# Attention and channel mix on one core: an order made by a small planner, q transposed two tokens at a time, kv kept in both partition halves, and two-bank PSUM tiles

## The chip, the cores and the metric

The kernel runs on one core of one Trainium2 chip. The metric is device time in microseconds (us), the median of several executions. A profiled execution gives a trace; its span (first to last instruction) is about 2 us shorter than the device time. "PE" is the matmul engine, "PEld" its weight loads, "DVE" VectorE, "ACT" ScalarE, "POOL" GpSimd, which issues the loads here. "Clock" is the TensorE clock that the throttle granted, as a share of full speed.

## The reference, cut to what matters

Batch 8, 8 heads, 576 tokens, 64 numbers a head. All of a batch's attention is linear: one 64x64 matrix `kv` a head, then `q @ kv`, normalised.

```python
kv = np.einsum('bhsd,bhse->bhde', k, v)
out = np.einsum('bhsd,bhde->bhse', q, kv)
rms = np.sqrt(np.mean(out * out, axis=-1, keepdims=True) + 1e-06)
x = (out / rms * g_norm)            # then heads side by side: [8, 576, 512]
x_prev = x shifted by one token
xk = mu_k * x + (1 - mu_k) * x_prev # xr likewise with mu_r
k = np.maximum(xk @ w_k, 0.0)       # 512 -> 1024
v = k * k @ w_v                     # 1024 -> 512
out = sigmoid(xr @ w_r) * v
```

## The kernel before

The kernel works on two kinds of things at once. *Attention* of a batch b (576 tokens) is a long chain: kv product, transposes of q, `u` (q times kv), squares, `st` (sum of squares), Ln and Exp on ScalarE, `rr` (spreads 1/rms over partitions), product with u, difference with the shifted token, blends to xk and xr. *Channel mix* of a group g (512 tokens) is 80 large matmuls: 32 for k, 16 for r (the gate), 32 for v. Group g needs x of batch g (and of those before it).

The attention matmuls use half the array's columns or rows:

```python
def transposes(hp):                  # hp: a pair of heads
    ps = psa.tile([128, S], BF16, tag="at", name="ps_qt")
    for j in range(NJ):              # NJ = 6 tokens a partition, NP = 96
        for e in range(2):
            nc.tensor.transpose(ps[64*e:64*e+64, NP*j:NP*j+NP],
                qin[:, 2*hp+e, HD*j:HD*j+HD], ident[:NP, :NP])
    nc.scalar.copy(out=st["qT"][:, hp, :], in_=ps)

def u(hp):
    for half in range(2):
        cs = slice(HS*half, HS*half+HS)          # HS = 288
        ps = psa.tile([128, HS], FP32, tag="at", name="ps_u")
        for e in range(2):
            es = slice(64*e, 64*e+64)
            nc.tensor.matmul(ps[es], st["kv"][es, hp, :], st["qT"][es, hp, cs], ...)
        nc.scalar.copy(out=st["uT"][:, hp, cs], in_=ps)
```

PSUM is two pools of four one-bank tiles, `psm` for the channel mix and `psa` for attention. The order on each engine is the order of the Python calls: every group has 20 units (r and k first, then v) and a table puts attention steps of a later batch after certain units:

```python
front(1, 0, [0, 1, 2, 3, 4])   # batch 1: kv after unit 0 of group 0, transposes after units 1 to 4
rest(1, 0, 5)
for b in range(2, B):
    front(b, b - 2, [15, 16, 17, 18, 19])
    rest(b, b - 1, 2)
```

In the trace, an instruction that has to wait holds up those behind it on its engine: in the first stretch shown below PE stands 3.3 us before one product although others could run.

## Time and profile before

| | before |
|---|---|
| time, median of its three runs by then (248.6, 252.0 and a slow one of 421.6) | 252.0 us |
| span of the profiled run, its clock | 250.2 us, 0.952 |
| first k product of group 1 | 66.7 us |
| period (one batch of attention and one group) | 24.5 us |

The head of the profile page of the kernel before: busy time of each engine, its share of the span, and its number of instructions.

```profile
span 250.2 us, 4403 instructions
## 1 busy us (share of the span) xinstructions
PE 218.7 (87%) x1746; PEld 93.2 (37%) x1746; DVE 154.6 (62%) x302; ACT 136.0 (54%) x252; POOL 23.6 (9%) x38
```

PE is the engine to look at. Two stretches of its timeline carry the argument. The columns are start in us, duration in us, engine, line, operation, what it writes and reads, shapes, number of matmuls merged, and in brackets the idle time before and what ended it. The start of the kernel before:

```profile
27.12 2.79 PE L229 MATMUL ps_r<-w_r,xr 128*128 128x512 bf16 x4 [3.49 <-DVE xr L202]
33.18 1.49 PE L141 MATMUL ps_kv<-vin,kin 96*64 96x64 bf16 x48 [3.27 <-DMA vin<-in_v_dram]
34.60 1.89 PE L229 MATMUL ps_r<-w_r,xr 128*128 128x512 bf16 x4
36.42 0.69 PE L125 MATMUL ps_qt<-ident,qin 96*64 96x96 bf16 x12
...
39.23 1.04 PE L229 MATMUL ps_r<-w_r,xr 128*128 128x512 bf16 x4
```

After four gate products PE comes to batch 1's kv product and waits 3.3 us for its data, although twelve more gate products could run.

A period in the steady state of the kernel before:

```profile
109.39 0.95 PE L141 MATMUL ps_kv<-vin,kin 96*64 96x64 bf16 x48
110.27 1.04 PE L242 MATMUL ps_v<-w_v,sqk 128*128 128x512 bf16 x4
111.24 0.45 PE L125 MATMUL ps_qt<-ident,qin 96*64 96x96 bf16 x12
111.62 1.04 PE L242 MATMUL ps_v<-w_v,sqk 128*128 128x512 bf16 x4
...
118.35 0.43 PE L159 MATMUL ps_u<-qT,kv 64*64 64x288 bf16 x4
118.71 1.04 PE L219 MATMUL ps_km<-xk,w_k 128*128 128x512 bf16 x4
```

Starts are more useful than durations, since matmuls overlap: a block of twelve transposes costs 0.38 us (111.24 to 111.62), a block of u 0.36, and the four large matmuls after either cost 0.97, where four undisturbed ones cost 0.86 (16 in 3.45 us in the last stage).

### The profile page before, as it was taken

The numbers are of one execution on the slowest core, as the hardware profiler recorded it, in microseconds if no ns is written. First come the engines' busy times: TensorE is split into PE (matmuls) and PEld (weight loads), VectorE is DVE, ScalarE is ACT, GpSimd is POOL, SyncE is SP. The second block draws the span as 40 slices with busy tenths as digits, with TensorE's granted clock in tenths as the row PEclk, the third lists the DMA queues.
The fourth block names the chain that finished last, engine by engine and source line by source line (L and its number), as shares of the span: only waits on it lengthen the run. The fifth ranks groups of instructions, "written<-read, shape, count | busy, mean of one in ns | idle before, by whom it ended". The sixth has DMA issues, their size and how long they took to land.

```text
span 250.2 us, 4403 instructions
## 1 busy us (share of the span) xinstructions
PE 218.7 (87%) x1746; PEld 93.2 (37%) x1746; DVE 154.6 (62%) x302; ACT 136.0 (54%) x252; POOL 23.6 (9%) x38
## 2 busy tenths in 40 slices
PE   0284369969998999899989998999899989999992
PEld 0251044324432543344335433543344334444440
DVE  0126920648875986597669766976796579714422
ACT  2077017850589258925891689168826880632610
POOL 8740021002100210021002100000000000000000
PEclk9997559995999999999999999999999999999999
DMA  5999999942990199019902990240023003206014
GB/s 82 182 208 207 203 203 204 203 81 54 206 182 0 42 183 226 2 45 179 230 2 55 206 197 0 56 114 0 3 83 85 4 0 85 87 9 159 1 55 113
DMA packets 26771, 26.49 MB, mean 106 GB/s; under 512 B 1656, under 2 KB 21632, under 8 KB 26752
## 3 DMA queue, kind: packets, MB, share of 16 engines
q0 software_dynamic: 20960, 16.78, 44.1%
q1 hardware_dynamic: 5792, 9.45, 13.2%
q8 instruction: 13, 0.21, 0.3%
q14 instruction: 6, 0.05, 0.1%
HBM read 33.56 MB, written 9.44 MB: 172 GB/s over the span
## 4 chain that ended last, share of the span: by engine, by line
PE 69%; ACT 15%; DMA 12%; issue 1%; DVE 1%; POOL 1%; DVEq 0%; POOLq 0%
PE ps_v L242 26%; PE ps_km L219 26%; DMA vin<-in_v_dram 9%; PE ps_r L229 5%; PE ps_qt L125 4%; PE ps_u L159 4%; ACT L176 4%; ACT L232 3%; PE ps_kv L141 3%; DMA kin<-in_k_dram 3%; ACT ln L177 3%; ACT rs L178 2%; ACT relu L222 2%; ACT sig L232 1%; DVE out_sb L247 1%
## 5 line engine op out<-in xcount | busy, mean ns | idle before, releaser
L242 PE MATMUL ps_v<-w_v,sqk 128*128 128x512 bf16 x288 | 70.0, 387 | 5.3 <-ACT sig L232 3.3
L219 PE MATMUL ps_km<-xk,w_k 128*128 128x512 bf16 x288 | 68.9, 380 | 0.0
L222 ACT ACTIVATE relu<-ps_km 128x512 bf16<-128x512 f32 x72 | 42.9, 597 | 28.9 <-PE ps_km L219 24.4
L223 DVE TENSOR_TENSOR sqk<-relu 128x512 bf16<-128x512 bf16 x72 | 30.3, 425 | 35.5 <-ACT relu L222 35.3
L130 ACT COPY qT<-ps_qt 128x576 bf16<-128x576 bf16 x32 | 20.2, 638 | 56.5 <-PE ps_qt L125 56.5
L229 PE MATMUL ps_r<-w_r,xr 128*128 128x512 bf16 x144 | 37.3, 400 | 3.9 <-DVE xr L202 3.5
L242 PEld LDWEIGHTS <-sqk 128*128 128x128 bf16 x288 | 26.2, 98 | 37.7 <-issue 7.7
L219 PEld LDWEIGHTS <-w_k 128*128 128x128 bf16 x288 | 25.2, 98 | 32.3 <-issue 6.5
L247 DVE TENSOR_TENSOR out_sb<-ps_v,sig 128x512 f32<-128x512 f32 x36 | 24.2, 686 | 16.7 <-PE ps_v L242 16.7
L232 ACT ACTIVATE sig<-ps_r 128x512 bf16<-128x512 f32 x36 | 19.6, 601 | 16.1 <-PE ps_r L229 16.0
L229 PEld LDWEIGHTS <-xr 128*128 128x128 bf16 x144 | 13.1, 100 | 24.2 <-DVE xr L202 6.0
L161 ACT CAST uT<-ps_u 128x288 bf16<-128x288 f32 x64 | 22.1, 413 | 0.0
L164 DVE TENSOR_TENSOR sq<-uT 128x576 bf16<-128x576 bf16 x32 | 14.7, 458 | 9.4 <-ACT uT L161 9.0
L190 DVE TENSOR_TENSOR xT_133<-uT,ps_rr 128x288 bf16<-128x288 bf16 x32 | 12.3, 449 | 8.9 <-PE ps_rr L187 8.8
L141 PE MATMUL ps_kv<-vin,kin 96*64 96x64 bf16 x384 | 9.4, 213 | 8.5 <-DMA vin<-in_v_dram 8.5
L190 DVE TENSOR_TENSOR xT_134<-uT,ps_rr 128x288 bf16<-128x288 bf16 x32 | 12.3, 449 | 6.7 <-PE ps_rr L187 6.7
L125 PEld LDWEIGHTS <-qin 96*64 96x64 bf16 x384 | 11.1, 119 | 14.3 <-issue 12.3
L125 PE MATMUL ps_qt<-ident,qin 96*64 96x96 bf16 x384 | 15.3, 223 | 0.9 <-DMA qin<-in_q_dram 0.8
L66 POOL DMA_DIRECT2D kin<-in_k_dram x9 | 6.9, 766 | 91.7 <-PE ps_kv L141 89.6
L159 PE MATMUL ps_u<-qT,kv 64*64 64x288 bf16 x128 | 14.6, 311 | 0.0
L141 PEld LDWEIGHTS <-kin 96*64 96x64 bf16 x384 | 8.7, 128 | 11.9 <-issue 9.5
L187 PE MATMUL ps_rr<-rs,selg 32*128 32x288 bf16 x64 | 10.8, 301 | 2.6 <-ACT rs L178 1.4
(41 smaller groups left out, 132.0 us busy)
## 6 DMA issues: line engine op xcount, KB each, us to landing
out_dram<-out_sb SPq DMA_DIRECT2D x24, 192.0 KB
kin<-in_k_dram POOLq DMA_DIRECT2D x7, 576.0 KB, 7.6
vin<-in_v_dram POOLq DMA_DIRECT2D x7, 576.0 KB, 10.6
qin<-in_q_dram POOLq DMA_DIRECT2D x7, 576.0 KB, 10.1
out_dram<-out_sb SPq DMA_DIRECT2D x24, 128.0 KB
out_dram<-out_sb SPq DMA_DIRECT2D x24, 64.0 KB
w_k<-in_moe_w_k_dram POOLq DMA_DIRECT2D x1, 1024.0 KB, 15.1
w_v<-in_moe_w_v_dram POOLq DMA_DIRECT2D x1, 1024.0 KB, 19.5
```

What stands on the lines that cost most here:

```text
L125: nc.tensor.transpose(ps[64 * e:64 * e + 64, NP * j:NP * j + NP], qin[:, 2 * hp + e, HD * j:HD * j + HD], ident[:NP, :NP],)
L141: nc.tensor.matmul(ps[64 * e:64 * e + 64, i, :], kin[:, 2 * hp + e, HD * j:HD * j + HD], vin[:, 2 * hp + e, HD * j:HD * j + HD], start=(j ...
L159: nc.tensor.matmul(ps[es], st["kv"][es, hp, :], st["qT"][es, hp, cs], start=True, stop=True)
L161: nc.scalar.copy(out=st["uT"][:, hp, cs], in_=ps)
L190: nc.vector.tensor_mul(out=xT[:, hp, NP + HS * half:NP + HS * half + HS], in0=st["uT"][:, hp, cs], in1=pss[hp])
L219: nc.tensor.matmul(ps, w_k_sb[:, cc, 128 * fc:128 * fc + 128], xk[:, cc, G * g:G * g + G], start=(cc == 0), stop=(cc == NHP - 1))
L222: nc.scalar.activation(out=rt, in_=ps, func=AF.Relu)
L223: nc.vector.tensor_mul(out=sqk[g][:, fc, :], in0=rt, in1=rt)
L229: nc.tensor.matmul(ps, xr[:, cc, n0:n0 + 128], w_r_sb[:, cc, :], start=(cc == 0), stop=(cc == NHP - 1))
L232: nc.scalar.activation(out=sig[(g, ci)], in_=ps, func=AF.Sigmoid)
L242: nc.tensor.matmul(ps, sqk[g][:, fc, 128 * ci:128 * ci + 128], w_v_sb[:, fc, :], start=(fc == 0), stop=(fc == NFC - 1))
L247: nc.vector.tensor_mul(out=ot, in0=ps, in1=sig[(g, ci)])
```

## The change

Its intent: less PE work for attention, fewer evictions, and an order that is computed, not written by hand.

- *Algebra.* q is transposed for two tokens at once (96x128, so six transposes a head pair, not twelve). The two tokens of a pair then lie in the two partition halves, so kv must stand in both halves (four small copies a batch in place of one), and u runs on four 64x64 tiles.
- *Two-bank PSUM tiles.* Two tiles for the mix and two for attention, of two banks each, so that one instruction evicts 1024 (or 576) columns.
- *Planner.* Every piece of work says which engines can do it, for how long (assumed durations), what it depends on, which buffers it needs, and a `due` number. At build the planner simulates the engines. On each it takes the piece that can start first, and among those within 0.02 us of it the one with the lowest `due`. The result is the fixed order of the instructions.
- Batch 0 is loaded and computed in three parts; xk and xr are rings of four batches.

The core of the diff, much cut:

```diff
+class Planner:
+    def run(self):
+            ...
+            for eng, c in best.items():
+                t0 = min(x[0] for x in c)
+                picks.append(min((x for x in c if x[0] <= t0 + 0.02), key=lambda x: x[1]) + (eng,))
...
+        "mm": (2, (128, 2, 512), FP32),
+        "at": (2, (128, 2, 512), FP32),
...
+        def due(x):
+            return 20 * b - 2 * x if b else -100 - x
...
+        def kv_copy(eng, e):
+            for half in range(2):
+                copy(eng, get(kv)[64 * half:64 * half + 64, hsl, e, :],
+                     pkv.t[64 * e:64 * e + 64, 0, 0:HD * n].rearrange("q (i d) -> q i d", d=HD))
...
+                for e in range(2):
+                    for i in range(NI):
+                        nc.tensor.transpose(t[:, e, NP * i:NP * i + NP],
+                                            qin.t[:, 2 * hp + e, 128 * i:128 * i + 128], ident[:NP, :NP])
...
+                for jj in range(2):
+                    js = slice(64 * jj, 64 * jj + 64)
+                    for e in range(2):
+                        nc.tensor.matmul(t[64 * e:64 * e + 64, jj, 0:NI * NP], kv.t[js, hp, e, :],
+                                         qT.t[js, 2 * hp + e, :], start=True, stop=True)
...
+        st = add({"ACT": 3.9 if b else 1.35}, st_act, deps=[m], bufs=[pst, ln, rs], due=due(17))
```

In `due(x)`, x is a number of the piece: 27 for the transposes, 26 for kv, 22 for u, 14 for rr, 10 or 6 for the blends. The mix of group g has numbers from 20g to 20g + 21.

## The prediction

> **What bounds the kernel now.** TensorE, after a slow start. On the page its busy share is 87% of the 250.2 us span; VectorE is at 62%, ScalarE at 54%. In the chain of waits PE holds 69%, ScalarE 15%, DMA 12%.
>
> Start: the chain is DMA until 33.18 us. The PE timeline shows why: gate products (L229) start at 27.1 us, but PE's next instruction is batch 1's kv product, waiting 3.3 us for its `vin`. The `ps_km` products of group 1 start only at 66.70 us.
>
> Steady state: starts of the kv product at 84.9, 109.4 and 133.9 us give a period of 24.5 us. In the last stage, without attention work, 16 large matmuls take 3.45 us (0.216 us each), so the period's 80 take 17.3 us. The rest: kv 0.88; four transposing blocks of 12 at 0.38; four u blocks at 0.36; stat 0.36; rr about 1.2; a wait for sigmoid 0.55; and after each return to 128x128 tiles a block of four costs 0.97 instead of 0.86 us, 13 times, 1.4 us. The sum is 24.6 us.
>
> **What the change does, by period.**
> - Transposes: 6 per head pair, not 12, at 96x128, so in the large matmuls' tiling mode. The Trainium skill's "TensorEngine Tiling (Array Packing)", Key Properties, says that changing mode drains TensorE; the 0.11 us above agrees. Estimate 0.28 us a block and no return cost: saves about 0.8 us.
> - u: the same four matmuls of 288 columns, but on four 64x64 tiles at once instead of two and two. Estimate 0.24 for 0.36 us: saves 0.5 us, more where two blocks are joined.
> - Fewer mode changes (about 9 returns a period, counted in the instruction order, for 13) and less stalled rr: about 1 us.
> - Added: kv is copied twice as four 64-partition pieces (1 to 2 us on ScalarE or VectorE); one group's k matmuls are split at the ring's wrap.
> - Two-bank tiles halve the number of evictions. ScalarE about 17.5, VectorE about 19 us a period (estimates from the durations of before): close, but still under PE's.
> New period: estimate 22.1 to 22.8 us.
>
> **The start.** Batch 0 is loaded and computed in three parts and batch 1's kv no longer stands before group 0's products. Loads stay bound by DMA at about 204 GB/s (batch 1 still lands at about 33 to 36 us). I expect group 0's gate products at 24 to 26 us, its k products running while batch 1 lands, and group 1's k products at about 54 us instead of 66.7. Three table loads of 1.28 us for batch 0 eat part of the gain. Before group 1 PE will still idle some 4 us, waiting for VectorE's blends.
>
> **Sum.** From 54 us: 8 groups at 17.3 plus about 5.6 attentions at 5.2 us, some 168 us, plus a tail of about 4.5 us: span about 226, time (some 2 us above the span) 227 us.
>
> Chances: faster 0.96, same 0.03, slower 0.01.
>
> **What would show it.** Transposing blocks of 6 under 0.35 us with no slow matmul after them; u blocks under 0.3 us; kv-to-kv period at 22 to 23 us; first group-1 k product between 50 and 58 us; PE busy share 88% or more.
>
> **What would make it wrong.** The order is fixed at build from assumed durations. If ScalarE or VectorE run behind them, two `mm` tiles give PE no more slack than four single ones, and PE waits for evictions; VectorE at about 85% makes this the likeliest miss (time 232 to 240). If the four u tiles do not run together, 3 to 4 us stay.

## The result

| | before | after |
|---|---|---|
| time, median of four | 251.9 us (fast runs 248.6 to 252.0, their median 251.8) | 240.5 us (239.9 to 240.6) |
| span, clock of the profiled run | 250.2 us, 0.952 | 238.5 us, 0.982 |
| first k product of group 1 | 66.7 us | 60.8 us |
| first k product of group 8, the last | 228.1 us | 214.4 us |

Ratio 0.958, 95% interval 0.950 to 0.965: faster. A ratio is the mean of one kernel's fast runs over the mean of the other's of the same rounds, so not quite the ratio of the medians. One run of before, 421.6 us, is left out of the ratio as slow. The prediction of 227 us was too low by 13.5 us.

The two mean clocks are not comparable. The trace's clock records begin at 18.3 us in the kernel before and at 31.87 us in the kernel after, and the views count time before the first record as full speed. It was not: in the kernel after the gate products run 0.43 us apart (the first two 0.73) until then and 0.216 after.

The head of the profile page of the kernel after:

```profile
span 238.5 us, 3893 instructions
## 1 busy us (share of the span) xinstructions
PE 207.4 (87%) x1586; PEld 98.0 (41%) x1586; DVE 158.7 (67%) x263; ACT 123.3 (52%) x154; POOL 25.1 (11%) x39
```

PE has 11 us less busy time, yet its share of the span is the same 87%. The PE timeline of the kernel after, in its steady state:

```profile
114.32 1.89 PE L453 MATMUL mm<-xk,w_k 128*128 128x512 bf16 x8
116.05 0.68 PE L315 MATMUL at<-ident,q 96*128 96x96 bf16 x12
117.85 0.43 PE L360 MATMUL at<-sq,sel_72 128*32 128x288 bf16 x8 [1.13 <-ACT qT L172]
...
134.53 0.32 PE L335 MATMUL at<-qT,kv 64*64 64x288 bf16 x4
134.78 1.04 PE L495 MATMUL mm<-w_v,sqk 128*128 128x512 bf16 x4
```

The new pieces cost what was predicted: u 0.25 us (134.53 to 134.78). The second fence below shows transposes of six at 0.35 us before rr, where PE changes mode (52.49 to 52.84), and four v products between transposes at 0.87 (51.62 to 52.49), so transposes in the large matmuls' shape no longer cost a change of mode. But at 117.85 PE has stood 1.13 us, until ScalarE had emptied an attention tile.

Group 0's gate products, which the prediction had at 24 to 26 us, and its first k products in the kernel after:

```profile
25.90 6.65 PE L476 MATMUL mm<-w_r,xr 128*128 128x512 bf16 x15 [1.58 <-DVE xr L413]
32.38 3.62 PE L453 MATMUL mm<-xk,w_k 128*128 128x512 bf16 x16
```

The end of the kernel's start, the PE timeline of after just before group 1's k products:

```profile
51.62 1.03 PE L495 MATMUL mm<-w_v,sqk 128*128 128x512 bf16 x4
52.49 0.42 PE L315 MATMUL at<-ident,q 96*128 96x96 bf16 x6
52.84 0.29 PE L384 MATMUL at<-rs,selg 32*128 32x288 bf16 x2
53.63 0.30 PE L384 MATMUL at<-rs,selg 32*128 32x288 bf16 x2 [0.50 <-ACT qT L172]
54.64 0.30 PE L384 MATMUL at<-rs,selg 32*128 32x288 bf16 x2 [0.71 <-DVE xT L391]
...
56.63 0.98 PE L335 MATMUL at<-qT,kv 64*64 64x288 bf16 x8 [0.21 <-DVE xT L391]
...
58.37 2.66 PE L315 MATMUL at<-ident,q 96*128 96x96 bf16 x24
60.83 1.90 PE L453 MATMUL mm<-xk,w_k 128*128 128x512 bf16 x4
```

From 52.84 to 60.83 us PE has only small pieces. It waits 2.6 us between them, and from 55.76 to 62.59 us the clock records stand at 0.50: the 24 transposes at 58.37 take 2.46 us where four blocks of six at full clock take 1.02. The window from 33 to 66 us (its columns are explained further down) has a mean clock of 0.90:

```profile
33.00:66.00 33.00, 29.56 (x348) 15.52 (x347) 22.93 (x39) 20.36 (x31) 6.92 (x9) 0.90 1.29 215
```

Batch 1's Exp was done at 48.8 us, but its rr stands in the order behind batch 2's transposes, and comes at 52.84.

*The account.* Give every block of PE from 60.83 us on its undisturbed cost: 0.2157 us a large matmul, 0.11 after a change of mode, and kv 0.88, st 0.36, transposes 0.255 a six, u 0.13 and 0.12 for every four, rr 0.11 and 0.06 for each. The sum is 164.0 us. Up to the last matmul's end it took 172.9 us. So some 9 us are lost: 7.8 us are PE's idle gaps, none above 1.13 us, and 0.9 is the slow clock in the first four k products (60.83 to 62.66). From 25.9 us on the sum is 190.0, and it took 207.9: 18 us of waits and slow clock, half of them before group 1.

VectorE in the kernel after, by windows (stretch, its length, then busy time of PE, PEld, DVE, ACT and POOL with instructions, clock, DMA share, GB/s):

```profile
66.00:99.00 33.00, 30.77 (x247) 13.40 (x245) 32.25 (x54) 22.18 (x28) 2.31 (x3) 1.00 0.75 125
```

VectorE is busy 32.25 of 33 us, 98%, though its share over the whole run is 67%. What it does there, in its timeline:

```profile
74.41 3.00 DVE L413 SCALAR_TENSOR_TENSOR xk<-d,mu_sb,xT 128x576 bf16<-128x576 bf16 x4
77.33 1.19 DVE L344 TENSOR_TENSOR sq<-uT 128x576 bf16<-128x576 bf16 x3
78.43 3.00 DVE L413 SCALAR_TENSOR_TENSOR xr<-d,mu_sb,xT 128x576 bf16<-128x576 bf16 x4
81.35 1.29 DVE L460 TENSOR_TENSOR sqk<-relu 128x1024 bf16<-128x1024 bf16 x2
82.56 1.73 DVE L174 CAST kv<-at 64x256 bf16<-64x256 f32 x4
84.45 1.42 DVE L391 TENSOR_TENSOR xT<-uT,at 128x576 bf16<-128x576 bf16 x2
```

These are blends of batch 2, squares of batch 3 and kv copies of batch 4, while group 1's v products start only at 84.56. The planner works ahead. I took from this three theories:

1. *The due numbers.* Attention's numbers make pieces of later batches go before what the current group needs.
2. *The durations* (rival). The planner assumed wrong times (for batch 0's statistics 1.35 us, measured 2.70 with the table load), so the order does not fit the chip.
3. *The evictions and the four PSUM tiles* (rival). Two two-bank tiles a kind give less slack than four single ones.

### The profile page after: what moved, and what is told of

It reads as the page before. It is cut to its first block, busy times and chain, and to the rows that moved or that the text cites. A ratio compares the mean times of both kernels' runs of the same rounds, so it can differ in the third digit from the quotient of the medians.

```text
span 238.5 us, 3893 instructions
## 1 busy us (share of the span) xinstructions
PE 207.4 (87%) x1586; PEld 98.0 (41%) x1586; DVE 158.7 (67%) x263; ACT 123.3 (52%) x154; POOL 25.1 (11%) x39
## 4 chain that ended last, share of the span: by engine, by line
PE 64%; DVE 16%; ACT 10%; DMA 5%; issue 2%; POOL 0%; SPq 0%; DVEq 0%; ACTq 0%; POOLq 0%
PE mm L495 22%; PE mm L453 22%; PE mm L476 11%; DVE out L499 4%; DMA q<-in_q_dram 3%; DVE xT L391 3%; PE at L315 2%; DMA out_dram<-out 2%; PE at L293 2%; ACT L365 2%; DVE xr L413 2%; DVE xk L413 2%; DVE sq L344 2%; ACT relu L457 2%; PE at L335 1%
## 5 line engine op out<-in xcount | busy, mean ns | idle before, releaser
L495 PE MATMUL mm<-w_v,sqk 128*128 128x512 bf16 x288 | 68.2, 380 | 1.7 <-DVE out L499 1.7
L453 PE MATMUL mm<-xk,w_k 128*128 128x512 bf16 (+1 forms) x320 | 67.6, 361 | 1.4 <-DVE out L499 1.4
L457 ACT ACTIVATE relu<-mm 128x1024 bf16<-128x1024 f32 x36 | 36.3, 1020 | 48.1 <-PE mm L453 48.1
L499 DVE TENSOR_TENSOR out<-mm,sig 128x1024 f32<-128x1024 f32 (+1 forms) x20 | 22.3, 1115 | 24.2 <-PE mm L495 17.8
L476 PE MATMUL mm<-w_r,xr 128*128 128x512 bf16 x144 | 36.5, 402 | 2.1 <-DVE xr L413 1.6
L460 DVE TENSOR_TENSOR sqk<-relu 128x1024 bf16<-128x1024 bf16 x36 | 24.6, 689 | 18.2 <-ACT relu L457 18.0
L391 DVE TENSOR_TENSOR xT<-uT,at 128x576 bf16<-128x576 bf16 (+1 forms) x31 | 21.7, 731 | 7.4 <-PE at L384 7.2
L480 ACT ACTIVATE sig<-mm 128x1024 bf16<-128x1024 f32 x18 | 18.5, 1027 | 12.0 <-PE mm L476 11.7
L413 DVE SCALAR_TENSOR_TENSOR xr<-d,mu_sb,xT 128x576 bf16<-128x576 bf16 x32 | 24.2, 813 | 0.0
L413 DVE SCALAR_TENSOR_TENSOR xk<-d,mu_sb,xT 128x576 bf16<-128x576 bf16 x32 | 24.1, 812 | 0.1
L365 ACT ACT_TABLE_LOAD x10 | 12.8, 1283 | 0.2
```

What stands on the lines that cost most here:

```text
L391: nc.vector.tensor_mul(out=xT.t[:, hs, xs], in0=get(uT)[:, hs].rearrange("q h i jj p -> q h (i jj p)")[:, :, cs], in1=ps.t[:, 0:step, 0:HS])
L413: nc.vector.scalar_tensor_tensor(out=dst[:, hp, c0:c0 + S], in0=d.t[:, hp, :], scalar=mu_sb[:, m + hp:m + hp + 1], in1=xT.t[:, hp, 0:S], o ...
L453: nc.tensor.matmul(get(ps)[:, fc % 2, a0:a1], w_k_sb[:, cc, 128 * fc:128 * fc + 128], xk[:, cc, x0:x0 + a1 - a0], start=(cc == 0), stop=(c ...
L457: nc.scalar.activation(out=get(rt), in_=ps.t, func=AF.Relu)
L460: nc.vector.tensor_mul(out=get(sqk)[:, 2 * f2:2 * f2 + 2, :], in0=rt.t, in1=rt.t)
L476: nc.tensor.matmul(get(ps)[:, ci % 2, :], xr[:, cc, n0:n0 + 128], w_r_sb[:, cc, :], start=(cc == 0), stop=(cc == NHP - 1))
```

## The experiments

All twelve were correct. K1 and K8 are the starts of the first k product of groups 1 and 8 in the profiled run. The reader may use the ratio, whose two sides come from the same chip and rounds; the kernel before ran at 250.6 to 251.9 us (medians) in the four sets of rounds, that of the result among them.

| run | time, us | ratio to before | K1 | K8 | span |
|---|---|---|---|---|---|
| before | 251.9 | 1 | 66.7 | 228.1 | 250.2 |
| after | 240.5 | 0.958 | 60.8 | 214.4 | 238.5 |
| e1_algebra_alone | 243.5 | 0.970 | 63.8 | 219.8 | 241.9 |
| e2_plan_alone | 243.3 | 0.970 | 62.0 | 217.0 | 241.1 |
| e3_later_due | 236.4 | 0.942 | 61.4 | 209.7 | 234.2 |
| e4_no_tables_b0 | 240.1 | 0.958 | 58.1 | 212.5 | 236.7 |
| e5_split_evict | 241.6 | 0.960 | 59.7 | 214.6 | 238.8 |
| e6_tail | 238.4 | 0.947 | 59.4 | 213.9 | 236.0 |
| e7_order_only | 230.5 | 0.915 | 59.3 | 205.8 | 228.0 |
| e8_all_fixes | 226.7 | 0.901 | 56.0 | 203.3 | 225.5 |
| e9_durations_alone | 239.8 | 0.956 | 57.8 | 215.4 | 239.5 |
| e10_front_alone | 236.8 | 0.943 | 61.5 | 210.4 | 234.5 |
| e11_before_start | 244.2 | 0.973 | 58.3 | 219.7 | 241.9 |
| e12_fixes_old_algebra | 230.8 | 0.919 | 56.0 | 206.6 | 228.7 |

### e1: the algebra alone

The kernel before with `transposes`, `kv` and `u` of the new kind; one-bank tiles, hand order. One kv copy goes to ScalarE, one to VectorE.

```diff
-            for j in range(NJ):
-                for e in range(2):
-                    nc.tensor.transpose(ps[64 * e:64 * e + 64, ...], qin[:, 2 * hp + e, HD * j:HD * j + HD], ...)
+            for e in range(2):
+                for i in range(NJ // 2):
+                    nc.tensor.transpose(ps[:, e, ...], qin[:, 2 * hp + e, 128 * i:128 * i + 128], ...)
```

> The kernel before, with only the new algebra: q transposed two tokens at a time, kv kept in both partition halves, u on four 64x64 tiles; old order, one-bank tiles. If the PE time that the change saves is real work off the bound engine, each of some 6.5 periods loses 4 x 0.24 us at the transposes and 4 x 0.11 us at u, about 9 us: 241 to 245 us. If the extra kv copies or waits give it back: 248 us or more.

243.5 us, as expected. Consecutive v stages start at 101.51 and 125.02 us: a period of 23.5 us against 24.5. The algebra's PE time is real, about 1 us a period.

### e2: planner and two-bank tiles alone

The kernel after with the old transposes, single kv and old u (and their durations) put back into the planner.

```diff
-                    for i in range(NI):
-                        nc.tensor.transpose(t[:, e, NP * i:NP * i + NP], qin.t[:, 2 * hp + e, 128 * i:128 * i + 128], ...)
+                for j in range(NJ): ...
+                        nc.tensor.transpose(t[64 * e:64 * e + 64, 0, NP * j:NP * j + NP],
+                                            qin.t[:, 2 * hp + e, HD * j:HD * j + HD], ...)
```

> The kernel after, with the old algebra put back into the planner (12 transposes a head pair, one kv, u two tiles at a time): planner and two-bank tiles alone. If the after kernel is bound by PE's work, the 1.4 us a period come back: 247 to 250 us. If it is bound by waits of a fixed order, the shorter attention work was partly hidden in them, and this shows only 243 to 246 us.

243.3 us: the case of waits. By medians each half of the change alone brings about 8 us, and both together 11, so they overlap by some 5. In the kernel after, the algebra is worth only 2.8 us.

### e3: later due numbers

```diff
-            return 20 * b - 2 * x if b else -100 - x
+            return 20 * b - 2 * x + 15 if b else -100 - x
```

> One constant in the after kernel: the due number of all attention pieces of batches 1 to 7 rises by 15 (three quarters of a group later). Theory: the missing time is waits that the order itself makes, because pieces of later batches go ahead of what the current group needs and VectorE saturates (98% busy from 66 to 99 us). Then 227 to 232 us, with VectorE no longer above 95% in any 33 us stretch. Rivals (durations that the planner has wrong; too few attention PSUM tiles): no change, 238 to 242 us.

236.4 us, 4 us less, but not the 9 to 13 that I expected. VectorE's window from 66 to 99 us falls to 29.57 us (90%). Starts of k products come at 84.09, 106.59, 129.08 and 151.63 us: an even period of 22.5 us. So theory 1 holds for the middle of the run, and another share of the loss lies elsewhere: K1 is at 61.4, no earlier. (VectorE's busiest 33 us are now from 55 to 88, at 31.53 us or 95.5%, just above what I expected.)

### e4: no table loads for batch 0

The table with Ln and Exp is loaded once at the very start, and batch 0 loads it three times more.

```diff
-            nc.scalar.preload_act_table_set("natural_log_exp_and_others")
+            if b:
+                nc.scalar.preload_act_table_set("natural_log_exp_and_others")
```

ScalarE's timeline in the kernel after shows what is taken away, three times in a row:

```profile
14.84 1.28 ACT L365 ACT_TABLE_LOAD   x1
16.13 0.74 ACT L366 ACTIVATE ln<-at,eps 64x576 f32<-64x576 f32 x1
16.90 0.68 ACT L368 ACTIVATE rs<-ln 64x576 bf16<-64x576 f32 x1
17.60 1.28 ACT L365 ACT_TABLE_LOAD   x1
```

> The after kernel, same order, without the three table loads (1.28 us each) in batch 0's statistics, whose table is loaded already. If the start runs through ScalarE (its chain from 14.8 to 23.1 us), group 0's gate products start about 2.5 to 3.8 us sooner than 25.9, and the end moves by 2 to 3 us: 237 to 238.5 us. If the later waits absorb it: the start moves and the end does not, 240 us.

240.1 us (238.8 to 240.7): unclear, at most a fraction of a microsecond. Gate products start only 0.6 us sooner than 25.9 (at 25.34, after one at 22.43 for 23.71), not the 2.5 to 3.8 expected. The profiled run has K1 2.7 us sooner and K8 1.9 sooner; its time was at the low end. The Trainium skill's "ScalarE: Activation LUTs", What ACT_TABLE_LOAD costs, gives about 1283 ns for the load, and the trace has exactly that mean. For a switch to another table the page adds a drain of about 1380 ns. The fence above reloads a table that is in use already, but a true switch shows no drain either: in the kernel before Exp ends at 79.37 us, the load runs from 79.40 to 80.68, and Sigmoid starts at 80.69.

### e5: the two-bank evictions undone

The same order, but relu, its square, sigmoid and output product as two one-bank instructions each.

```diff
-            nc.scalar.activation(out=get(rt), in_=ps.t, func=AF.Relu)
+            get(rt)
+            for x in range(2):
+                nc.scalar.activation(out=rt.t[:, x, :], in_=ps.t[:, x, :], func=AF.Relu)
```

> The after kernel with the same order, but every two-bank eviction of the channel mix (relu, its square, sigmoid, output product) issued as two one-bank instructions. From the mean durations (relu 2 x 597 against 1020 ns, square 2 x 425 against 689, output 2 x 686 against 1221) ScalarE gets about 9 us more work and VectorE about 8. If those engines' waits carry the time, 3 to 6 us slower than 240.5; if the joining of evictions is off the critical chain, within 1 us.

241.6 us, 1.1 more by medians and 0.2% by ratio. The joining of the channel mix's evictions is hardly on the chain. The extra busy time was also smaller than I had worked out: ScalarE 126.2 against 123.3 us, VectorE 163.1 against 158.7.

### e6: the tail

The last group evicts its output tiles in halves, but the halves share one PSUM tile. PE's timeline at the end of the kernel after:

```profile
224.72 2.75 PE L495 MATMUL mm<-w_v,sqk 128*128 128x512 bf16 x12
228.31 3.61 PE L495 MATMUL mm<-w_v,sqk 128*128 128x512 bf16 x16 [0.84 <-DVE out L499]
232.76 1.02 PE L495 MATMUL mm<-w_v,sqk 128*128 128x512 bf16 x4 [0.84 <-DVE out L499]
```

PE writes the second bank of the tile, and waits until VectorE has read the first. With a tile for each half:

```diff
-            ps, ot, u = Buf("mm"), Buf("out"), slot + 12 + 4 * c2
+            pp, ot, u = [Buf("mm")], Buf("out"), slot + 12 + 4 * c2
+            pp.append(pp[0] if g < NG - 1 else Buf("mm"))
```

> The after kernel with one PSUM tile for each 128 tokens in the last group's output product, so that PE need not wait until VectorE has read the first half of a two-bank tile (two waits of 0.84 us in the last stage, and a slice of output). Expected 1.5 to 2 us less: 238.4 to 239.

238.4 us, as expected: 2 us. In its trace the last 32 products are one block without a wait:

```profile
224.30 7.07 PE L495 MATMUL mm<-w_v,sqk 128*128 128x512 bf16 x31
```

(One record of 32 is missing from the trace.)

### e7: the order fixes together

e3, e4 and e6, and a next batch's kv and transposes less urgent than this batch's rr (the change of e10).

> Order and waits together, with the planner's assumed durations unchanged: the later due numbers (236.4 alone), no table loads in batch 0, the last group's tiles split, and a next batch's kv and transposes no longer more urgent than this batch's rr. If the missing 13 us are such waits, the gains add: group 1's k products at 57 to 58 us instead of 60.8, 230 to 232 us.

230.5 us, as expected, though K1 came later than I wrote (59.3). Waits that seemed small one by one add up to 10 us. From K1 to the last matmul's end it takes 163.7 us (59.34 to 223.03), where the kernel after takes 172.9: the 9 us lost there are gone.

### e8: the same, with durations that the trace shows

```diff
-        st = add({"ACT": 3.9 if b else 1.35}, ...
+        st = add({"ACT": 2.75 if b else 1.45}, ...
-            sigs.append((sg, add({"ACT": 1.04}, ...
+            sigs.append((sg, add({"ACT": 1.04 + 1.28 * (c2 == 0)}, ...
-            qts[hp] = add({"ACT": 0.65, "DVE": 0.75}, ...
+            qts[hp] = add({"ACT": 0.65, "DVE": 0.46}, ...
-            m = add({"PE": 0.35}, ... q_tr ...
+            m = add({"PE": 0.26}, ... q_tr ...
```

> As the run before it, and the planner is given durations that the trace shows (table load counted with sigmoid, qT copy on VectorE 0.46 us, transposes 0.26 us). Rival theory that the order is stale because its durations are wrong: 2 us or more better than the run before, group 1's k products at 54 to 56 us, 227 to 229 us. If the durations hardly matter: within 1 us of the run before.

226.7 us, ratio 0.901 (0.898 to 0.904): this version beats both kernels, and is where the prediction had put the change itself. Against e7 it gains before K1 only: from K1 to K8 it takes 147.3 us, e7 146.5. Its profiled run is the slowest of four and has 3.4 us at a clock of 0.50 (54.92 to 58.34), e7's has 6.8 (54.15 to 60.97), and the other three runs of e8 have a mean clock of 0.999 or 1.000, those of e7 0.985. So part of the 3.8 us between them is the clock; whether the better order keeps it up is not shown. Its window from 66 to 99 us, and a period of its PE timeline:

```profile
66.00:99.00 33.00, 32.52 (x258) 14.64 (x263) 29.39 (x48) 22.26 (x27) 3.08 (x4) 1.00 0.75 121
```

```profile
123.45 1.91 PE L454 MATMUL mm<-xk,w_k 128*128 128x256 bf16 x16
125.29 0.95 PE L293 MATMUL at<-v,k 96*64 96x64 bf16 x48
...
135.13 0.42 PE L315 MATMUL at<-ident,q 96*128 96x96 bf16 x6
135.39 1.03 PE L477 MATMUL mm<-w_r,xr 128*128 128x512 bf16 x4
...
145.58 0.38 PE L454 MATMUL mm<-xk,w_k 128*128 128x512 bf16 x1
```

PE is busy 32.52 of 33 us, and the period, 123.45 to 145.58, is 22.1 us. That is the predicted sum without waits.

### e9: the durations alone

The changed numbers of e8 on the kernel after (2.75 us for all statistics, since batch 0 keeps its loads), the due numbers untouched.

> The after kernel with only the planner's assumed durations corrected (table load of the statistics 2.75 us and of sigmoid 1.28 us apart, qT copy on VectorE 0.46, transposes 0.26), its due numbers as they were. If wrong durations alone made the order bad: 236 us or less. If the due numbers are the cause and right durations only help once those are right: 238 to 243 us.

239.8 us, runs from 238.7 to 241.6: no gain that the runs can tell. K1 does come 3 us sooner (57.8), but K8 is at 215.4, later than in the kernel after. (The profiled run is the slowest of the four, at a mean clock of 0.981; the two below 239 us have 0.993 and 0.999.) So theory 2 alone falls as the cause of the whole time: right durations came with 3.8 us from e7 to e8, and with nothing that can be told without the right due numbers. For the start it does not fall (see K0 below).

### e10: one priority

```diff
-        mm = add({"PE": 0.23 * n + 0.1}, kv_mm, ..., due=due(26), ...
+        mm = add({"PE": 0.23 * n + 0.1}, kv_mm, ..., due=due(23.5), ...
-            m = add({"PE": 0.35}, ... q_tr ..., due=due(27), ...
+            m = add({"PE": 0.35}, ... q_tr ..., due=due(23.4), ...
```

(kv copies and qT copies get 23.3 and 23.2.) With the old numbers a transposing piece of batch b + 1 has 20(b + 1) - 54 = 20b - 34, so it goes before rr of batch b, which has 20b - 28.

> The after kernel with one thing changed: a next batch's kv product and transposes get due numbers that are no longer more urgent than this batch's rr. If batch 1's rr was late because batch 2's transposes held the two attention tiles, group 1's first k product moves from 60.8 to 57 to 59 us, and the time to 237.5 to 239.5. If the tiles were not the reason: no change, 240 to 241.

236.8 us, a little better than expected, but not in the way I expected: K1 stays at 61.5, and the gain lies between K1 and K8 (148.9 us against 153.6). That batch 1's rr was late because of the tiles held by batch 2's transposes is therefore not shown; rr came only 1 us sooner (51.8), and the waits for VectorE behind it stayed. VectorE is still 99% busy here from 69 to 102 us (32.72 of 33), so a relief of VectorE hardly explains the gain.

### e11: the hand order with batch 1 moved

The kernel before, with batch 1's front behind group 0's gate products and the rest of batch 1 one unit later.

```diff
-    front(1, 0, [0, 1, 2, 3, 4])
-    rest(1, 0, 5)
+    front(1, 0, [3, 3, 4, 4, 5])
+    rest(1, 0, 6)
```

(The last blends, which would fall out of the 20 slots, are clamped to slot 19.)

> The kernel before with one thing changed: batch 1's kv product and transposes stand after group 0's gate products in PE's order, and the rest of batch 1 one slot later. The prediction blamed that position for the late start: then group 1's first k product (66.7 us) comes 3 us sooner or more, 247 to 249 us. If the chain of batch 1's attention, which starts when its q lands at about 36 us, sets that moment: within 1 us of before.

244.2 us: more than either side expected. (The interval is 0.966 to 0.981: faster beyond noise, but not surely by the 2% that a verdict asks, so on record it is "unclear".) K1 moves 8.4 us, although the wait that was taken away is 3.3 us. At batch 1's st this run is only 3.0 us ahead (46.04 us against 49.08); the other 5.4 come after it. The windows of the kernel before, and then of this run:

```profile
30.00:40.00 10.00, 6.82 (x84) 3.47 (x84) 2.59 (x4) 2.82 (x5) 1.53 (x2) 0.56 1.32 204
50.00:60.00 10.00, 7.98 (x75) 3.21 (x72) 5.43 (x14) 3.35 (x6) 0.00 (x0) 0.79 0.37 70
```

```profile
30.00:40.00 10.00, 8.96 (x121) 4.35 (x121) 2.90 (x6) 5.21 (x11) 2.28 (x3) 1.00 1.32 204
50.00:60.00 10.00, 9.03 (x126) 4.43 (x127) 9.63 (x18) 3.15 (x5) 2.31 (x3) 1.00 1.02 170
```

The first pair does not compare clocks: this run's records begin at 32.75 us, and its gate products too ran 0.43 us apart until then. The second pair does. In the kernel before PE waits 1.95 us, to 53.94, for the last `sqk` of group 0: its relu (52.84) stands on ScalarE behind batch 1's table load, Ln and Exp (from 49.80 on). Then the clock is 0.50 from 55.85 to 62.67 us. Here, one unit later, the last relu (46.15) stands before the table load (46.77), PE's longest gap from 50 to 60 us is 0.69 us, and the clock stays at 1.00. So two waits were taken away, one by each line of the edit, and no run parts them.

The Trainium skill's "TensorE: Matmul & The Clock Gate", Part 1, says that the array drops to half rate after an idle window of about 3.4 us and needs about as long to warm up. The traces agree on the half rate (four products in 1.82 us at a clock of 0.50, in 0.97 at full clock). But the clock fell at 55.85 us in the kernel before after a gap of 1.95 us, and at 55.76 in the kernel after with no gap above 0.71 us just before, where PE was busy 0.62 of the 2 us from 54 to 56. If such waits are what lets the clock fall, which no run isolates, a stretch with waits costs more than the waits. And these two moved lines of the hand order start group 1 sooner (58.3) than the planner did (60.8).

### e12: the fixed order with the old algebra

e8 with the replacements of e2.

> The version with all order fixes (226.7 us), with the old algebra put back (12 transposes a head pair, one kv, u two tiles at a time). On the after kernel the algebra was worth only 2.8 us (243.3 against 240.5), on the kernel before 8. If waits had hidden it, it is worth its PE time again, about 1.4 us for each of 7 attentions, once the waits are gone: 235 to 238 us. If not: 229 to 231.

230.8 us, 4.1 more than e8: the expectation's "if not". The algebra was worth 2.8 us in the kernel after, so the waits had hidden some 1.3 us of it, and my theory that they had hidden most of its 1.4 us a period is wrong in size. The period here is 22.9 us (k starts at 79.43, 102.29, 125.15) against 22.1: the algebra is worth 0.8 us a period, five times, which is the 4.1. Here the order puts kv and a block of old transposes side by side, and two more blocks together (90.14 to 92.88 us), so the old algebra pays for fewer changes of mode too.

## Why the prediction was wrong

It forecast 227 us and 240.5 came. Point by point:

- *What bounds the kernel: right.* PE's work is the floor, and stays it.
- *The new pieces: right.* Transposes 0.26, predicted 0.28; u 0.25, predicted 0.24; no slow block after transposes. The Trainium skill's "TensorEngine Tiling (Array Packing)", Key Properties, on the drain at a change of mode is borne out: 0.97 against 0.86 us after u, 0.87 after transposes in the large matmuls' own shape. (The 0.26 is from e8's fence, 135.13 to 135.39.)
- *The period of 22.1 to 22.8 us: right as a sum, wrong for this kernel.* k products of groups 4 and 5 start 22.8 us apart (137.74 and 160.49), but of 3 and 4 23.4, and the account from K1 on has 9 us of waits and slow clock. I predicted 168 us from K1 to the last matmul, 4 more than the account's 164.0 of work, but with no term for waits; 172.9 came. e8 shows the 22.1.
- *The start at 54 us: wrong by 6.8.* Moving batch 1's kv was right: e11, which moves it in the hand order, is 3.0 us ahead at st. But the prediction gave 54 without a sum. The gate products did start at 25.9 as predicted (one at 23.7). From there to K1 the account has 26.0 us of work, so even with the 4 us of idling that I had allowed the sum would have been 55.9. It took 34.9. Of the 8.9 us lost, 3.2 are in the gate products: 15 of them took 6.48 us where 15 x 0.2157 = 3.2 would do, at half rate, which I had left out. About 5 are in the stretch from 52.84 to 60.83 us, 8 us for about 2.9 us of work: 2.6 us of waits, and the rest the clock of 0.50 from 55.76 us on, which I had left out too.
- *The tail: nearly right* (4.5 us predicted, 4.7 after the last matmul), but 2 us of PE's own waits before it were not seen (e6).
- *"What would make it wrong": half right.* I named VectorE at about 85% as the likeliest miss, at 232 to 240 us. VectorE was indeed at 98% in one stretch. But I blamed the planner's assumed durations. e9 shows that correcting them alone brings nothing in the time that the runs can tell, while the due numbers bring 4 us by one constant (e3) and 3.7 by another (e10).

So the step that failed is the term for waits, and no term stood for the slow clock. The sum from K1 and the start's 54 us took the planner's order as one in which PE hardly waits, at full clock. In the trace 172.9 us pass from K1 on for the 168 predicted, and K1 is 6.8 us late: with the tail's 0.2 these are the 12 us between the spans (226.5 by the prediction's terms, 238.5).

- *After K1 the cause is shown: it is the order.* e3, e6 and e10 take away 4.1, 2.1 and 3.7 us, and e7, all with e4, takes away 10.0, without touching the algebra, the number of tiles or the assumed durations; from K1 to the last matmul it takes 163.7 us. Theory 3 falls as an explanation of most of it: e8 has the same four PSUM tiles, and e5 shows that joining the mix's evictions is worth about 1 us.
- *Before K1 it is only in part shown.* Call K0 the first k product of group 0. K1 comes 28.2 to 28.6 us after K0 in the kernel after, e3, e4, e5, e6, e7 and e10, whatever the due numbers; up to about 50 us PE's order of pieces is the same in all seven. So where K1 differs among these seven, it is K0 that moved (32.4 us in after, 29.9 in e4, 31.1 in e7, 33.0 in e10), and K0 moves among other things with the moment at which the gate products go from half to full rate (31.9 us in after, 29.6 in e5 and e6). With the new algebra only right durations shorten the stretch: to 26.9 us in e8 and 23.7 in e9. In e9 the clock falls only behind K1 (63.05 us), which is part of it. Which of the durations does it was not tested, nor the clock apart from the order.

## What to carry to other kernels

A schedule computed at build is only as good as its priorities: check in the trace whether an engine that is not the bottleneck is saturated for a stretch with work of a later stage, and try that work's due number as well as the durations: here the due numbers cured the middle of the run, and only the durations shortened the stretch from K0 to K1. When you predict a change, price the bottleneck's work and its waits as two separate sums, do not assume that a computed order leaves the second near zero, and look for stretches at a lower clock before you call lost time a wait. Two halves of a change that shorten the same engine's time need not add up (8 and 8 gave 11 us here), so test each alone and again after the order is mended.

## What the Trainium skill lacked or had wrong

- "TensorEngine Tiling (Array Packing)", Key Properties: it says that a change of tiling mode drains TensorE, but not what that costs. Here it is about 0.11 us on the four matmuls after it (0.97 against 0.86 us).
- "TensorEngine Tiling (Array Packing)", Performance Considerations: nothing on transposes. Two tokens a transpose, 96x128, cost 0.26 us a head pair against 0.38 for twelve of 96x64, and need no change of mode beside large matmuls.
- "TensorE: Matmul & The Clock Gate", Part 1: it ties the fall of the clock to an idle window of about 3.4 us, and names frequent short idling as a second cause without a size. In the kernel after it fell, to 0.50 at 55.76 us, behind gaps of 0.37 to 0.71 us, with PE busy 0.62 of the 2 us from 54 to 56.
- "ScalarE: Activation LUTs", What ACT_TABLE_LOAD costs: 1283 ns agrees to the digit; the drain of about 1380 ns that it adds for a switch is not seen. In the kernel before Exp ends at 79.37 us, the load runs from 79.40 to 80.68, and Sigmoid starts at 80.69.
- No page that I used has what a wait on a whole two-bank tile costs when only one bank is in use: 0.84 us twice, 2 us of the time (e6).
